# Row maxima of the attention scores taken as minima of negated scores

## The chip, the cores and the metric

The kernel runs on one core of one Trainium2 chip. The metric is the device time of one execution in microseconds (us). Engines: TensorE (PE; its weight loads are PEld), VectorE (DVE), ScalarE (ACT), GpSimd (POOL) and SyncE (SP), which issues nearly all DMAs here.

## The reference, cut to what matters

Local and global attention, then a two-layer MoE block, then a soft MoE. Only the local attention is touched by the change; with B = 4, H = 8, 512 local and 32 global keys, head dimension 64:

```
def sm(s):
    s = s - np.max(s, axis=-1, keepdims=True)
    e = np.exp(s)
    return e / (np.sum(e, axis=-1, keepdims=True) + 1e-09)
s_ll = scale * q_l @ k_l^T            # masked to |i - j| <= 32 with -1e9
s_lg = scale * q_l @ k_g^T
out_l = sm(concat([s_lg, s_ll])) @ concat([v_g, v_l])
out_g = sm(scale * q_g @ [k_g; k_l]^T) @ [v_g; v_l]
x = concat([out_g, out_l])            # 2176 rows of 512
h = x @ w_in;  g = max(0.01 h, h);  x = g @ w_out      # w_in 512 x 2048
# soft MoE over x: logits x @ phi, two softmaxes, 8 experts (w1, w2)
```

## The kernel before, in words

The attention works on 16 pairs of heads (4 batches, 4 pairs each). For a pair, `a_T` transposes queries and keys (kT, qT) and builds overlapping key windows (kw, L405 and L406), `a_S` makes the scores and the exponentials, `a_E` transposes the exponentials (etp, copied to eT at L477), and `a_V` multiplies by the values (po) and scales into xn (L501). A score tile is 128 queries by 128 keys (a window of 96 local keys and the 32 global ones); a pair has 8 of them, 4 for each head of the pair.

In `a_S` a tile goes through three steps: the scores by TensorE (L434, into sc); a fused instruction of VectorE that adds the mask, writes the sum to se and keeps the row maximum in mx (L446); and the exponential by ScalarE (L454), with the negated maximum nmx as its bias and the row sum kept in sm. Between the second and the third, one negation for the four tiles of a head turns mx into nmx (L452).

The MoE block takes token tiles of 128 rows: `b_X` transposes xn and splits it into a high and a low part (xxh, xxl; xqn and xkn for the third tile, L665 and L666), and `b_H` multiplies by w_in (hp, L689), 12 matmuls for each quarter f of 512 columns. The product with w_out is folded into the router: `p_items` transposes 16 pieces of w_out (wotp, L345), copies them (wt, L347) and multiplies them by phi (ptps, L354). `b_L` transposes the activations (gtp, L726), whose copies are gT (L728).

Both weights arrive as 64-bit integers' words. `fetch` loads a piece of 128 x 512 into a ring of four buffers (rraw, L233), and `convert` makes it 32-bit: two steps on ScalarE (L250, L251), two on VectorE (L253, L257) and one on GpSimd (L261), behind which the buffer is free again. A piece of w_in is then split into wi by a cast on ScalarE (L307) and a subtraction on GpSimd or VectorE (L308).

What sets the order: the program is written as lists of items that `merge` interleaves by weights written in the source, and the framework's scheduler then orders the instructions of each engine by a simulated timeline of its own. Each engine runs its own list strictly in order. In the opening (the attention of the first batch, with the pieces of w_in) TensorE also runs matmuls of the identity (`warm`, L85) that compute nothing.

Of the kernel before, what the change touches and what calls it, by code (L numbers as in the profile page):

```python
# [8 lines left out]
F32 = mybir.dt.float32  # L9
# [4 lines left out]
AF = mybir.ActivationFunctionType  # L14
ALU = mybir.AluOpType
# [5 lines left out]
def kernel(  # L21
# [15 lines left out]
    nc = tc.nc  # L37
# [4 lines left out]
    P = 128  # L42
    NT = S // P
# [7 lines left out]
    scale = 1.0 / float(D) ** 0.5  # L51
# [7 lines left out]
    def bank(tag, name, bufs):  # L59
        return ps.tile([P, 512], F32, tag=tag, name=name, bufs=bufs)  # L60
# [9 lines left out]
    with tc.tile_pool(name="id", bufs=1) as idp:  # L70
# [6 lines left out]
        out=s44[:, 0, :], in_=ident.rearrange("p (g s) -> p s g", g=4), axis=AX.X, op=ALU.add  # L77
# [5 lines left out]
    def warm(t):  # L83

        nc.tensor.matmul(  # L85
            t, identr, identr.unsqueeze(1).to_broadcast([P, 4, P]), start=True, stop=True
        )
# [24 lines left out]
    sa = actx.enter_context(tc.tile_pool(name="sa", bufs=2))  # L112
# [23 lines left out]
    for r in range(2):  # L136
        nc.gpsimd.affine_select(
            out=em4[:, r, :], in_=em4[:, r, :], compare_op=ALU.is_ge, fill=0.0,
# [3 lines left out]
            out=em4[:, r, :], in_=em4[:, r, :], compare_op=ALU.is_ge, fill=0.0,  # L142
# [269 lines left out]
    def win(u):  # L412
        return min(max(u - 1, 0), NW - 1)
# [3 lines left out]

    def a_S(b, i):
        qt, kw = qT.pop((b, i)), kwin.pop((b, i))
        mx = sa.tile([P, 2, NT], F32, tag="mx", name="mx", bufs=2)  # L420
        nmx = sa.tile([P, 2, NT], F32, tag="nmx", name="nmx", bufs=2)
        sm = sa.tile([P, NT, 2], F32, tag="sm", name="sm", bufs=2)
        rs = sa.tile([P, NT, 2], F32, tag="rs", name="rs", bufs=2)
        es = []
        bks = [bank("sc", f"sc{e}", 2) for e in range(2)]
        if b == 0:
            for bk in bks:
                warm(bk)
        seq_ = [(T, u, e) for T in range(NT) for u in range(4) for e in range(2)]
        for T, u, e in seq_ if b > 1 else sorted(seq_, key=lambda x: x[2]):  # L430
            U = 4 * T + u
            if True:
                if True:
                    last_a[0] = nc.tensor.matmul(  # L434
                        bks[e][32 * u:32 * u + 32, P * T:P * T + P],
                        qt[64 * e:64 * e + 64, 32 * U:32 * U + 32],
                        kw[win(U) // (NW // 2)][64 * e:64 * e + 64, win(U) % (NW // 2), :],
                        start=True, stop=True,
                    ).ins
        for e in range(2):  # L440
            bk = bks[e]
            s = sa.tile([P, S + SG], F32, tag="se", name="se", bufs=4)[:, 0:S].rearrange(
                "p (t k) -> p t k", t=NT
            )
            for T in range(NT):
                nc.vector.tensor_tensor_reduce(  # L446
                    out=s[:, T, :], in0=bk[:, P * T:P * T + P],
                    in1=mask[:, 0 if T == 0 else 2 if T == NT - 1 else 1, :],
                    scale=1.0, scalar=-3.0e38, op0=ALU.add, op1=ALU.max,
                    accum_out=mx[:, e, T:T + 1],  # L450
                )
            nc.vector.tensor_scalar_mul(nmx[:, e], mx[:, e], -1.0)  # L452
            for T in range(NT):
                exp_last[0] = nc.scalar.activation(  # L454
                    out=s[:, T, :], in_=s[:, T, :], func=AF.Exp,
                    bias=nmx[:, e, T:T + 1], accum_out=sm[:, T, e:e + 1],
                ).ins
            es.append(s)
        nc.vector.tensor_scalar_add(sm, sm, 1e-9)
        nc.vector.reciprocal(rs, sm)  # L460
        sc[b, i] = (es, rs)
# [166 lines left out]
    def step(n):  # L628

        b, i = order[n]  # L630
        last = i == NP - 1
        e = (0.9, lambda: a_E(b, i))
        v = (1.6, lambda: (a_V(b, i), None if n < NP else load_vn(b) if i == NP - 2 else load_v(n + (1 if last else 2))))
        ns = [(2.7, lambda: a_S(*order[n + 1]))] if n + 1 < NN else []
        nt = [(0.9, lambda: T_(n + 2))] if n + 2 < NN else []
        if not last:
            gs = [(2.2, lambda: g_S(b))] if i == NP - 2 else []
            return ns + [e] + gs + nt + [v]
        gv = (2.1, lambda: (g_V(b), load_v(n + 2) if b else None))
        return [e, (0, lambda: None), v, (1.1, lambda: g_E(b))] + ns + nt + [gv]  # L640
# [368 lines left out]
    g_prep(kgn, kgT, 1.0)  # L1009
    T_(0)  # L1010
    a_S(*order[0])
    T_(1)
    st0, st1, st2, st3 = (step(n) for n in range(NP))
# [37 lines left out]
    with tc.issue_after(raw_last[0]):  # L1051
        load_vn(0)
    s4, s5, s6, s7 = (step(n) for n in range(NP, 2 * NP))
    h3 = [(2.6, lambda f=f: b_H(3, f)) for f in range(NQ)]
    merge(pit, hs[3] + [(2.1, lambda: (g_V(0), load_v(NP)))] + [
        (0.9, lambda: T_(NP)), (2.7, lambda: a_S(*order[NP])), (0.9, lambda: T_(NP + 1))
    ] + s4[:2] + [(0.5, lambda: b_X(3))] + h3[:2] + s4[2:-1])
    pctx.close()
# [30 lines left out]
    for n, t in enumerate(wo2):  # L1089
        nc.sync.dma_start(  # L1090
            out=t, in_=wo_f[512 * n:512 * n + 512, :].rearrange("(k p) f -> p k f", p=P)
# [217 lines left out]
    for m, (c0, c1) in enumerate(((0, CL), (CL, 512))):  # L1309
        W = c1 - c0  # L1310
        sop = bank(("po", "sm")[m], "sop", 1)[:, 0:W]
        for k in range(KF):
# [8 lines left out]
            out=so[:, c0:c1], in0=so0[:, c0:c1], in1=sop, op=ALU.add  # L1321
# [3 lines left out]
        if m == 0:  # L1325
# [3 lines left out]
            out=sst[64:128, c0:c1], in0=sp[64:128], in1=sst[64:128, c0:c1], op=ALU.subtract  # L1329
# [4 lines left out]
        for n, ts in enumerate(order2):  # L1334
# [11 lines left out]
            if len(ts) == 1:  # L1346
# [3 lines left out]
                    out=out.rearrange("(b r) c -> b r c", b=B)[:, 0:SG, c0:c1], in_=ob  # L1350
                )
            else:
                ob = obp.pop(0).rearrange("p (t c) -> p t c", c=W)
                copy(ob, opv)
                b, T = seq[ts[0]]
                r0 = ROWS * b + SG + P * T
                (nc.scalar if m and nop % 2 else nc.sync).dma_start(
                    out=out[r0:r0 + G * P, c0:c1].rearrange("(t p) c -> p t c", p=P), in_=ob
# [36 lines left out]
```

## Time and profile before

| what | us |
|---|---|
| median of 3 runs | 491.11 (490.76 to 493.39) |
| the profiled execution | 492.57 |
| its span, first to last instruction | 490.8 |
| TensorE busy | 458.0 (93%) |
| VectorE busy | 274.7 (56%) |
| ScalarE busy | 232.7 (47%) |
| GpSimd busy | 160.1 (33%) |

The granted clock of TensorE is 0.974 of full speed over the span, and 0.66 from 25 to 50 us. A row of the timeline gives the start, the duration of the row, the engine, the line, what is written from what, and in brackets how long the engine was idle before and what ended that. Durations of neighbours overlap, since an instruction starts before the last one's end is through.

### The profile page before, as it was taken

How to read it: one execution, taken by the hardware profiler on the slowest of the kernel's cores; microseconds unless marked ns; L12 is line 12 of the kernel's file. 1: busy time of each engine (PE TensorE's matmuls, PEld its weight loads, DVE VectorE, ACT ScalarE, POOL GpSimd, SP SyncE). 2: the span in 40 equal slices, each digit the busy share in tenths (PEclk: the TensorE clock that was granted, in tenths of full speed). 3: DMA queues.
4: the chain of work that ended last, by engine and by line, in shares of the span. 5: the costliest groups of instructions: out<-in, count | busy, mean ns of one | idle time of the engine just before them, and what ended most of it. 6: DMA issues, size and time to landing. Idle time of an engine off the chain costs nothing.

```text
span 490.8 us, 13457 instructions
## 1 busy us (share of the span) xinstructions
PE 458.0 (93%) x5341; PEld 318.5 (65%) x5341; DVE 274.7 (56%) x880; ACT 232.7 (47%) x678; POOL 160.1 (33%) x281
## 2 busy tenths in 40 slices
PE   7968789998989999999999999999999999999982
PEld 5646568675767666776777776777777777743341
DVE  4676879488557676466554656435755542242223
ACT  4666889477854445444155526123533343321021
POOL 2044887333310202642515251515766630000000
PEclk9985899999999999999999999999999999999998
DMA  9989688499665565443450221229720049999997
GB/s 178 220 201 244 206 271 331 158 294 294 206 164 109 132 130 93 95 104 92 99 107 1 59 46 16 87 99 397 278 86 1 2 164 346 392 348 398 348 308 248
DMA packets 111990, 90.23 MB, mean 184 GB/s; under 512 B 75256, under 2 KB 94392, under 8 KB 111928
## 3 DMA queue, kind: packets, MB, share of 16 engines
q1 hardware_dynamic: 110024, 88.33, 61.8%
q10 hardware_dynamic: 1904, 1.05, 0.8%
q8 instruction: 42, 0.69, 0.6%
q14 instruction: 20, 0.16, 0.1%
HBM read 76.68 MB, written 8.65 MB: 174 GB/s over the span
## 4 chain that ended last, share of the span: by engine, by line
PE 74%; DMA 9%; ACT 6%; SPq 4%; DVE 4%; issue 1%; POOL 1%; DVEq 0%; ACTq 0%; POOLq 0%
PE hp L689 37%; DMA rraw<-in_moe_w_in_dram 5%; PE gtp L726 4%; PE sc L434 3%; PE up L810 3%; PE ehp L1259 3%; PE po L493 3%; PE lg L740 3%; PE etp L473 2%; DMA rraw<-in_moe_w_out_dram 2%; PE sop L1293 1%; SPq L162 1%; ACT se L454 1%; PE gpo L579 1%; PE qTp L390 1%
## 5 line engine op out<-in xcount | busy, mean ns | idle before, releaser
L689 PE MATMUL hp<-wi,xxh 128*128 128x512 f32 x512 | 166.9, 407 | 1.3 <-ACT xxh L665 1.3
L689 PEld LDWEIGHTS hp<-wi,xxh 128*128 128x128 f32 x512 | 91.7, 190 | 28.3 <-issue 8.2
L717 POOL COPY g<-gb 32x256 f32<-32x256 f32 x206 | 82.6, 401 | 81.4 <-DVE gb L708 54.3
L689 PE MATMUL hp<-wi,xxl 128*128 128x512 f32 x256 | 101.4, 397 | 0.2 <-DVE xxl L666 0.2
L696 ACT ACTIVATE g<-hp 128x512 f32<-128x512 f32 x60 | 35.3, 595 | 56.2 <-PE hp L689 54.2
L454 ACT ACTIVATE se<-se,nmx 128x128 f32<-128x128 f32 x128 | 49.6, 390 | 22.5 <-DVE nmx L452 22.5
L689 PEld LDWEIGHTS hp<-wi,xxl 128*128 128x128 f32 x256 | 48.5, 189 | 13.0 <-issue 1.7
L200 POOL COPY vw<-vw 32x1664 f32<-32x1664 f32 x10 | 15.8, 1576 | 79.6 <-DMA vw<-in_v_g_dram 26.7
L446 DVE CUSTOM_DVE_ANT_0 se<-sc,mask 128x128 f32<-128x128 f32 x128 | 28.8, 283 | 12.1 <-PE sc L434 12.0
L261 POOL TENSOR_TENSOR wn<-wn,rraw 128x512 int32<-128x512 int32 x16 | 22.9, 1436 | 36.9 <-DVE wn L257 31.1
L708 DVE STREAM_TRANSPOSE gb<-g 128x512 f32<-128x512 f32 x32 | 22.2, 702 | 18.7 <-ACT g L696 13.4
L434 PE MATMUL sc<-kw,qT 64*32 64x128 f32 x1024 | 29.2, 283 | 1.5 <-ACT rraw L251 0.6
L261 POOL TENSOR_TENSOR wo<-wo,rraw 128x512 int32<-128x512 int32 x12 | 15.7, 1310 | 33.0 <-DVE wo L257 9.6
L434 PEld LDWEIGHTS sc<-kw,qT 64*32 64x32 f32 x1024 | 19.9, 109 | 9.5 <-issue 5.4
L493 PE MATMUL po<-vw,eT 128*32 128x64 f32 x1024 | 23.8, 228 | 1.2 <-issue 1.0
L477 DVE COPY eT<-etp 128x512 f32<-128x512 f32 x28 | 18.6, 684 | 10.0 <-PE etp L473 10.0
L454 ACT ACTIVATION_READ_ACCUMULATOR se<-se,nmx 128x1 f32 x128 | 24.1, 188 | 0.0
L473 PE MATMUL etp<-identr,se 128*128 128x128 f32 x128 | 23.1, 301 | 0.3
L493 PEld LDWEIGHTS po<-vw,eT 128*32 128x32 f32 x1024 | 17.8, 113 | 8.1 <-issue 6.8
L405 DVE COPY kw<-kT 128x672 f32<-128x672 f32 x32 | 19.8, 652 | 2.9 <-ACT kT L394 2.7
L251 ACT ACTIVATE rraw<-rraw 128x512 int32<-128x512 uint32 x28 | 18.7, 677 | 5.0 <-DMA rraw<-in_moe_w_out_dram 3.8
L473 PEld LDWEIGHTS etp<-identr,se 128*128 128x128 f32 x128 | 16.0, 148 | 6.6 <-ACT se L454 2.8
(228 smaller groups left out, 765.3 us busy)
## 6 DMA issues: line engine op xcount, KB each, us to landing
ew<-in_moe_w_dram SPq DMA_DIRECT2D x23, 1024.0 KB, 8.2
rraw<-in_moe_w_in_dram SPq DMA_DIRECT2D x16, 512.0 KB, 6.1
ew<-in_moe_w_dram SPq DMA_DIRECT2D x15, 512.0 KB, 8.8
vw<-in_v_l_dram SPq DMA_DIRECT2D x60, 112.0 KB, 3.3
rraw<-in_moe_w_out_dram SPq DMA_DIRECT2D x12, 512.0 KB, 6.6
wo_f<-wo SPq DMA_DIRECT2D x16, 256.0 KB, 3.8
vn<-in_v_l_dram SPq DMA_DIRECT2D x4, 1024.0 KB, 6.3
wo<-wo_f SPq DMA_DIRECT2D x4, 1024.0 KB, 7.7
```

Of the source, the lines that this page charges most:

```text
L261: nc.gpsimd.tensor_tensor(out=di, in0=di, in1=m, op=ALU.add)
L405: nc.vector.tensor_copy(kw[:, :, 0:96], src)
L434: last_a[0] = nc.tensor.matmul(bks[e][32 * u:32 * u + 32, P * T:P * T + P], qt[64 * e:64 * e + 64, 32 * U:32 * U + 32], kw[win(U) // (NW / ...
L446: nc.vector.tensor_tensor_reduce(out=s[:, T, :], in0=bk[:, P * T:P * T + P], in1=mask[:, 0 if T == 0 else 2 if T == NT - 1 else 1, :], sca ...
L454: exp_last[0] = nc.scalar.activation(out=s[:, T, :], in_=s[:, T, :], func=AF.Exp, bias=nmx[:, e, T:T + 1], accum_out=sm[:, T, e:e + 1],).ins
L473: last_a[0] = nc.tensor.transpose(pt[:, P * T:P * T + P], es[e][:, T, :], ident).ins
L493: last_a[0] = nc.tensor.matmul(pov[32 * u:32 * u + 32, T, e, :], ets[e][:, 32 * U:32 * U + 32], vw[:, win(U), e, :], start=True, stop=True ...
L689: nc.tensor.matmul(hp, a[:, k, :], w[c][:, k, :], start=(k == 0 and n == 0), stop=(k == KD - 1 and n == 2),)
L696: nc.scalar.activation(out=gs, in_=hp, func=AF.Prelu, alpha=0.01)
L708: nc.vector.transpose(out=gb[:, f % 2], in_=gs)
L717: copy(dst[32 * c:32 * c + 32, :, a], src[32 * a:32 * a + 32, :, c])
L726: nc.tensor.transpose(pt[:, P * c:P * c + P], g[:, o:o + P], ident)
```

## The change

The fused instruction gets a scale of -1 and a minimum in place of the maximum: it writes the negated masked scores, and the minimum of these, kept directly in nmx, is the negated maximum. The tile mx and the 32 negations (16 pairs, 2 heads each) go. The exponential multiplies its input by -1.

```
--- before.py
+++ after.py
@@ -417,7 +417,6 @@
 
     def a_S(b, i):
         qt, kw = qT.pop((b, i)), kwin.pop((b, i))
-        mx = sa.tile([P, 2, NT], F32, tag="mx", name="mx", bufs=2)
         nmx = sa.tile([P, 2, NT], F32, tag="nmx", name="nmx", bufs=2)
         sm = sa.tile([P, NT, 2], F32, tag="sm", name="sm", bufs=2)
         rs = sa.tile([P, NT, 2], F32, tag="rs", name="rs", bufs=2)
@@ -446,13 +445,12 @@
                 nc.vector.tensor_tensor_reduce(
                     out=s[:, T, :], in0=bk[:, P * T:P * T + P],
                     in1=mask[:, 0 if T == 0 else 2 if T == NT - 1 else 1, :],
-                    scale=1.0, scalar=-3.0e38, op0=ALU.add, op1=ALU.max,
-                    accum_out=mx[:, e, T:T + 1],
+                    scale=-1.0, scalar=3.0e38, op0=ALU.add, op1=ALU.min,
+                    accum_out=nmx[:, e, T:T + 1],
                 )
-            nc.vector.tensor_scalar_mul(nmx[:, e], mx[:, e], -1.0)
             for T in range(NT):
                 exp_last[0] = nc.scalar.activation(
-                    out=s[:, T, :], in_=s[:, T, :], func=AF.Exp,
+                    out=s[:, T, :], in_=s[:, T, :], func=AF.Exp, scale=-1.0,
                     bias=nmx[:, e, T:T + 1], accum_out=sm[:, T, e:e + 1],
                 ).ins
             es.append(s)
```

The order of the instructions changes as well, since the scheduler orders the program anew. Line numbers behind L420 are lower by one or two in the changed program.

The first place is ScalarE, 60 to 64 us, the arrival of the last pieces of w_in. cv is a piece's high word, g the activation of the first tile, xqn the high part of the third token tile. Before:

```order
L307 CAST wi<-wn 128x512
L251 ACTIVATE rraw<-rraw 128x512
L250 ACTIVATE cv<-rraw 128x512 x2
L251 ACTIVATE rraw<-rraw 128x512
L307 CAST wi<-wn 128x512
L696 ACTIVATE g<-hp 128x512
L665 ACTIVATE xqn<-xtp 128x512
L307 CAST wi<-wn 128x512 x2
```

and of the change:

```order
L307 CAST wi<-wn 128x512
L251 ACTIVATE rraw<-rraw 128x512
L250 ACTIVATE cv<-rraw 128x512
L694 ACTIVATE g<-hp 128x512
L250 ACTIVATE cv<-rraw 128x512
L251 ACTIVATE rraw<-rraw 128x512
L663 ACTIVATE xqn<-xtp 128x512
L307 CAST wi<-wn 128x512 x2
```

The cast L307 that stood ahead of xqn now stands behind it, and the activation is one step nearer.

The second place is VectorE, 42 to 53 us. The rows with cv are pieces 5, 6 and 7 of w_in; xn is the product of the attention of the third and fourth head pair. Before:

```order
L257 SCALAR_TENSOR_TENSOR wn<-rraw,wn 128x512
L501 TENSOR_TENSOR xn<-po,rs 128x4x128
L459 TENSOR_SCALAR sm<-sm 128x8
L477 COPY eT<-etp 128x512
L253 TENSOR_SCALAR cv<-cv 128x512
L460 RECIPROCAL rs<-sm 128x8
L257 SCALAR_TENSOR_TENSOR wn<-rraw,cv 128x512
L253 TENSOR_SCALAR cv<-cv 128x512
L257 SCALAR_TENSOR_TENSOR wn<-rraw,cv 128x512
L253 TENSOR_SCALAR cv<-cv 128x512
L501 TENSOR_TENSOR xn<-po,rs 128x4x128
L257 SCALAR_TENSOR_TENSOR wn<-rraw,cv 128x512
```

and of the change:

```order
L257 SCALAR_TENSOR_TENSOR wn<-rraw,wn 128x512
L475 COPY eT<-etp 128x512
L457 TENSOR_SCALAR sm<-sm 128x8
L458 RECIPROCAL rs<-sm 128x8
L253 TENSOR_SCALAR cv<-cv 128x512
L499 TENSOR_TENSOR xn<-po,rs 128x4x128
L475 COPY eT<-etp 128x512
L257 SCALAR_TENSOR_TENSOR wn<-rraw,cv 128x512
L253 TENSOR_SCALAR cv<-cv 128x512
L257 SCALAR_TENSOR_TENSOR wn<-rraw,cv 128x512
L499 TENSOR_TENSOR xn<-po,rs 128x4x128
L253 TENSOR_SCALAR cv<-cv 128x512
```

The first shift (L253) of cv has moved ahead of the first xn, while its second step (L257) stays behind that and the copy eT.

The third place is ScalarE, 134 to 142 us, the last pieces of w_out; the exponentials are those of the seventh head pair. Before:

```order
L250 ACTIVATE wo<-rraw 128x512
L347 COPY wt<-wotp 128x512 x2
L454 ACTIVATE se,sm<-se,nmx 128x128 x4
L347 COPY wt<-wotp 128x512
L454 ACTIVATE se,sm<-se,nmx 128x128 x4
L728 COPY gT<-gtp 128x512 x2
L361 ACTIVATE pmat<-ptps 128x128
```

and of the change:

```order
L250 ACTIVATE wo<-rraw 128x512
L347 COPY wt<-wotp 128x512
L452 ACTIVATE se,sm<-se,nmx 128x128 x7
L347 COPY wt<-wotp 128x512
L452 ACTIVATE se,sm<-se,nmx 128x128
L726 COPY gT<-gtp 128x512 x2
L361 ACTIVATE pmat<-ptps 128x128
```

Before, four exponentials stood ahead of the last copy wt; now there are seven.

## Rows read from the trace of the kernel before

**Rows 1.** The page's first part: busy us, share of the span, instructions.
```profile
PE 458.0 (93%) x5341; PEld 318.5 (65%) x5341; DVE 274.7 (56%) x880; ACT 232.7 (47%) x678; POOL 160.1 (33%) x281
```

**Rows 2.** Busy time by stretch: length, engines' busy us (instructions), clock, DMA share, GB/s.
```profile
0.00:65.00 65.00, 51.05 (x658) 35.95 (x658) 43.34 (x145) 44.21 (x123) 26.93 (x37) 0.84 0.94 210
65.00:200.00 135.00, 129.72 (x1687) 92.41 (x1687) 94.96 (x295) 84.83 (x244) 44.70 (x42) 1.00 0.71 196
200.00:425.00 225.00, 224.41 (x2415) 164.60 (x2413) 115.42 (x392) 92.12 (x283) 88.48 (x204) 1.00 0.40 125
425.00:491.00 66.00, 52.77 (x584) 25.55 (x584) 20.95 (x51) 11.58 (x29) 0.00 (x0) 0.96 0.96 334
```

**Rows 3.** The timeline from 44 to 56 us, four engines, rows picked.
```profile
44.21 0.61 ACT L250 ACTIVATE cv<-rraw 128x512 f32<-128x512 f32 x1
...
46.59 0.69 DVE L501 TENSOR_TENSOR xn<-po,rs 128x512 f32<-128x512 f32 x1 [2.92 <-PE po L493]
...
48.45 0.69 DVE L253 TENSOR_SCALAR cv<-cv 128x512 uint32<-128x512 uint32 x1
...
49.10 0.65 ACT L250 ACTIVATE cv<-rraw 128x512 f32<-128x512 f32 x1 [1.53 <-DMA rraw<-in_moe_w_in_dram]
...
49.99 2.72 POOL L261 TENSOR_TENSOR wn<-wn,rraw 128x512 int32<-128x512 int32 x2 [2.72 <-DVE wn L257]
...
53.91 3.04 POOL L261 TENSOR_TENSOR wn<-wn,rraw 128x512 int32<-128x512 int32 x2
...
55.71 0.33 SPq L233 DMA_DIRECT2D rraw<-in_moe_w_in_dram  x1
```

**Rows 4.** Groups by line: busy us, mean ns of one; idle before, releaser.
```profile
L446 DVE CUSTOM_DVE_ANT_0 se<-sc,mask 128x128 f32<-128x128 f32 x128 | 28.8, 283 | 12.1 <-PE sc L434 12.0
...
L452 DVE TENSOR_SCALAR nmx<-mx 128x4 f32<-128x4 f32 x32 | 7.8, 258 | 0.2
...
L454 ACT ACTIVATE se<-se,nmx 128x128 f32<-128x128 f32 x128 | 49.6, 390 | 22.5 <-DVE nmx L452 22.5
```

**Rows 5.** The negation's line: durations in ns, least, median, longest.
```profile
L452 DVE TENSOR_SCALAR nmx<-mx x32: 149/164/1250, 14.5 to 295.3; 128x4 f32<-128x4 f32 x32
```

**Rows 6.** The timeline from 62 to 65 us, TensorE and ScalarE.
```profile
62.50 0.60 PE L607 MATMUL gtp<-identr,gn 128*128 128x128 f32 x4
62.77 0.60 ACT L307 CAST wi<-wn 128x512 fp32r<-128x512 f32 x1
63.28 0.59 ACT L696 ACTIVATE g<-hp 128x512 f32<-128x512 f32 x1
63.77 0.59 ACT L665 ACTIVATE xqn<-xtp 128x512 fp32r<-128x512 f32 x1
...
64.41 0.73 PE L689 MATMUL hp<-wi,xqn 128*128 128x512 f32 x2 [1.31 <-ACT xqn L665]
```

**Rows 7.** The timeline from 137 to 143 us, three engines.
```profile
137.82 1.08 PE L434 MATMUL sc<-kw,qT 64*32 64x128 f32 x32
...
139.52 0.59 ACT L347 COPY wt<-wotp 128x512 f32<-128x512 f32 x1
...
140.16 1.06 PE L354 MATMUL ptps<-wt,phis 128*32 128x128 f32 x26 [0.34 <-ACT wt L347]
...
141.17 0.69 DVE L501 TENSOR_TENSOR xn<-po,rs 128x512 f32<-128x512 f32 x1 [1.07 <-PE ptps L354]
...
141.78 0.68 DVE L728 COPY gT<-gtp 128x512 f32<-128x512 f32 x1
...
142.51 0.66 PE L726 MATMUL gtp<-identr,g 128*128 128x128 f32 x4 [1.29 <-DVE gT L728]
```

**Rows 8.** The timeline at 40 us, VectorE and ScalarE: a long negation.
```profile
39.83 1.21 DVE L452 TENSOR_SCALAR nmx<-mx 128x4 f32<-128x4 f32 x1
...
41.07 0.40 ACT L454 ACTIVATE se<-se,nmx 128x128 f32<-128x128 f32 x1 [1.40 <-DVE nmx L452]
```

**Rows 9.** The ring's sends of w_out from 90 to 125 us.
```profile
L233 SPq DMA_DIRECT2D rraw<-in_moe_w_out_dram x8: 328/372/1481, 93.3 to 123.5; - x8
```

More of the change, by code (lines that the diff above doesn't have):

```diff
@@ L419, in a_S @@
         qt, kw = qT.pop((b, i)), kwin.pop((b, i))
-        mx = sa.tile([P, 2, NT], F32, tag="mx", name="mx", bufs=2)
         nmx = sa.tile([P, 2, NT], F32, tag="nmx", name="nmx", bufs=2)
@@ L448, in a_S @@
                     in1=mask[:, 0 if T == 0 else 2 if T == NT - 1 else 1, :],
-                    scale=1.0, scalar=-3.0e38, op0=ALU.add, op1=ALU.max,
-                    accum_out=mx[:, e, T:T + 1],
+                    scale=-1.0, scalar=3.0e38, op0=ALU.add, op1=ALU.min,
+                    accum_out=nmx[:, e, T:T + 1],
                 )
-            nc.vector.tensor_scalar_mul(nmx[:, e], mx[:, e], -1.0)
             for T in range(NT):
                 exp_last[0] = nc.scalar.activation(
-                    out=s[:, T, :], in_=s[:, T, :], func=AF.Exp,
+                    out=s[:, T, :], in_=s[:, T, :], func=AF.Exp, scale=-1.0,
                     bias=nmx[:, e, T:T + 1], accum_out=sm[:, T, e:e + 1],
```

## The prediction

> **What bounds the kernel now.** I read the page's first part, then the busy time by stretch. TensorE is busy for 458.0 of 490.8 us [rows 1]. By stretch [rows 2] it lacks 13.95 us in the first 65, 5.28 from 65 to 200, 0.59 from 200 to 425, and the rest in the tail. Three quarters of the kernel is therefore matmul behind matmul, and what another engine saves beside a busy TensorE is worth nothing. The tail from 425 moves as a whole: DMA is at 0.96 there, but its weight loads go into buffers that TensorE's work frees. What this change can move is two things: when TensorE's steady stream begins, and how many short waits stand in it between 65 and 200. The part before 65 is held by the pieces of the first weight, which come by DMA through a ring of four buffers and are converted by ScalarE, VectorE and GpSimd in turn. I call them pieces 1 to 16; the one that ScalarE takes at 49.10 is piece 6, and the one at 44.21 piece 5 [rows 3].
>
> **What goes, and its price.** There are 32 negations, 7.8 us of VectorE time [rows 4], most of them 0.16 us long and one 1.25 [rows 5]. VectorE is busy for 274.7 us of the span [rows 1], so this is 3% of an engine with 216 us to spare. From 65 us on TensorE's matmuls cover it. With that cover gone the price would be the 7.8 us at most; I take zero.
>
> The trace shows neither of the new forms, the minimum in the reduction and the scale of -1 in the exponential. The nearest rows are the old forms, 128 each, of 0.283 and 0.390 us [rows 4], with the same operands and element counts. If each new form were 0.1 us off, either way, it would be 12.8 us on each of two engines that are half idle, again beside TensorE. I take no difference, and price even that at under 1 us either way, since only the opening would show it.
>
> A second effect: a tile's exponential now needs its own reduction alone, not the fourth of its group and a negation: one 0.16 and up to three reductions of 0.283 less, some 0.8 to 1.0 us earlier for a group's first exponential, where ScalarE is free. ScalarE waits 22.5 us for the negations in all [rows 4]; all but the opening's share of it lies beside a busy TensorE.
>
> **What moves.** The scheduler orders the program anew around these savings. I follow the two places where the waits of TensorE are longest.
>
> *The start of the stream.* TensorE ends a group of transposes at 63.10 (62.50 + 0.60) and waits 1.31 us for the copy xqn, the third token tile's high part, which ScalarE starts at 63.77 [rows 6]. Ahead of xqn on ScalarE, behind the arrival of piece 11, stand conversions, a cast (L307) and an activation. In the changed order that cast stands behind xqn. From its start at 62.77 to the next at 63.28 it is 0.51 us [rows 6]. Piece 11 itself was sent at 55.71, when GpSimd had freed piece 7's buffer, the first of the two in the row at 53.91; before that it did pieces 5 and 6 in 2.72 us from 49.99 on [rows 3]. Piece 5 came that late because its VectorE shift, at 48.45, stood behind the product xn, which had waited 2.92 us for TensorE; ScalarE had delivered the piece at 44.82 (44.21 + 0.61) [rows 3]. Now the shift stands ahead of xn, and the attention work before it has lost its negations, so piece 5 leaves GpSimd before piece 6, which lands at 49.10, needs it. Half of the 2.72, or 1.36 us, goes from GpSimd's list ahead of piece 7, but piece 6 passes VectorE no more than a few tenths sooner. So piece 11 is sent between 0 and 1.36 us earlier; I take 0.5, nearer the low end, because piece 6's landing is the nearest row. Together xqn is 1.0 us earlier. Bounds: at best the whole wait of 1.31 goes; at worst the four exponentials that now stand ahead of a conversion of piece 3 (4 x 0.390) push a later piece by 1.6. I take -1.0.
>
> *The end of the second weight's pieces, at 139 us.* TensorE waits 0.34 us for a copy wt and then 1.29 for a copy gT [rows 7]. Let E be 138.90, the end of the last score matmuls (137.82 + 1.08). Before, wt started after four exponentials, at E + 0.62, and the products that need it ran from E + 1.26. Now seven exponentials stand ahead of wt, and the seventh needs the third reduction of the last group: 3 x 0.283 after E, then 0.390 of its own and 0.59 of wt, so the products start at about E + 1.8, half a microsecond later. They take 1.06. Behind them on VectorE stand xn (0.69), two small steps (some 0.3, a sum and a reciprocal like those beside them) and gT (0.68) [rows 7], so gT is done at about E + 4.5. The transposes behind that wait ran from 142.51, with the next group able to follow at 143.17, or E + 4.3, and it is that next group which needs gT now. This place loses 0.2 us. Bounds: it gains the 1.63 of both waits if all is ready, and loses 1.0 if the two delays add. I take +0.2.
>
> *The other waits between 65 and 200.* 5.28 in all, less the 1.63 of that place, leaves 3.65 us. Their places keep their kind, but each hangs on an order that has changed. I see no sign: zero, with -3.65 and +3.65 as the ends.
>
> **The sum.** -1.0 + 0.2 = -0.8 us. The profiled execution took 492.57 us, its span of 490.8 and 1.8 around it, so 491.8 on its own terms. It lay 1.46 above the median of the runs, 491.11; for the median the forecast is 490.3.
>
> **A rule weighed.** One negation took 1.21 us where 0.16 is usual, and the exponential behind it waited 1.40 [rows 8]; the longest took 1.25 [rows 5]. The Trainium skill, page "SBUF — State Buffer", section "Who interferes with whom", says that a VectorE instruction in a two-port mode and a GpSimd instruction take an exclusive lock on a shared pair of ports, and the other blocks for the whole instruction. By that rule such a wait leaves with its instruction, and what stands next, if it is not of that kind, starts at once. By the rows alone the two cost 2.1 us (1.05 and 1.09) more than the others would.
>
> **Rivals.**
> *Faster: the two held negations were on the path.* If what delayed pieces 3 to 5 was those two, the start gains 2.1 us more: 488.2 us. For it: both lie before 41.1, in the stretch that ends TensorE's slow opening, and ScalarE's next work waited for one of them. Against it: ScalarE still waits 1.53 us at 49.10 for piece 6's DMA [rows 3], so a lead won before that is lost there, and the next copies on VectorE can be held in the same way. The same time comes out if over half of the 3.65 us of other waits goes.
> *Slower: exponentials hold back the second weight's pieces.* The place is 93 to 143 us, where 8 pieces of the second weight are sent between 93.3 and 123.5 [rows 9]. Exponentials that become ready one by one are now put ahead of conversions and of wt on ScalarE. If one piece misses its turn in the ring, TensorE waits for one spacing: 30.2 / 7 = 4.3 us, and with the terms above the time is 494.6. It decides from the point where a piece is later than the work that is queued ahead of its transposes. For it: TensorE waits for wt already at 140.16, so the reserve there is gone. Against it: the loads and conversions of this stretch keep their order but for a few places.
> *It does nothing:* negations off the path and an order of equal worth give 491.1, inside the forecast's own case.
>
> **Chances.** The forecast's case, 488.7 to 493.5, has 0.60; faster 0.22; slower 0.18. A measurement of this kernel tells about 0.5% (2.5 us) from no change, so these cases are also the three chances. The range, 487.5 to 494.6, takes in the points of both rivals; the terms' own ends (-1.31 - 1.63 - 3.65 and +1.6 + 1.0 + 3.65) reach a little further, and all of them at once I leave out.
>
> **What would show it.** Right: the third tile's first matmuls start near 63.4 in place of 64.41; TensorE's lack from 65 to 200 is again 4 to 7 us; 200 to 425 is as full as before; the two groups of reductions and exponentials last 0.28 and 0.39. Wrong: a start of that tile before 62 or after 65, a new wait of over 2 us between 93 and 143, or a minimum form that lasts longer than the maximum form.

## The result, and the profile after

The change makes the kernel slower. In the first comparison its median is 497.48 us (496.3 to 498.32, 4 runs) against 492.25 of before (490.76 to 493.39, 4 runs), a ratio of 1.0106 [1.0063, 1.0149]. Run again beside other kernels it is 497.01 against 492.21, 1.0082 [1.0054, 1.0110]. The forecast was 490.3, with 494.6 as the upper end of its range. The profiled execution took 496.3 us, its span 494.6; that is 3.7 us over before's profiled one, where the medians differ by 4.8 to 5.2, so the two profiles show a little less than the whole loss.

The page of the changed kernel, first part and the two groups that answer to [rows 1, 4]:

```profile
PE 458.9 (93%) x5341; PEld 319.8 (65%) x5341; DVE 268.5 (54%) x848; ACT 234.2 (47%) x678; POOL 158.6 (32%) x281
...
L452 ACT ACTIVATE se<-se,nmx 128x128 f32<-128x128 f32 x128 | 49.8, 392 | 19.8 <-DVE nmx L445 19.5
L445 DVE CUSTOM_DVE_ANT_0 se<-sc,mask 128x128 f32<-128x128 f32 x128 | 28.8, 284 | 13.1 <-PE sc L433 13.0
```

The negations are gone: VectorE has 848 instructions for 880 and 6.2 us less to do. The new forms last 0.284 and 0.392 us, the old ones 0.283 and 0.390. ScalarE even waits 2.7 us less for the row maxima. None of this is where the time went.

Busy time by stretch, columns as in [rows 2]:

```profile
0.00:65.00 65.00, 49.71 (x661) 35.68 (x662) 42.69 (x137) 45.01 (x125) 26.00 (x37) 0.87 0.97 215
65.00:200.00 135.00, 128.24 (x1620) 91.27 (x1619) 89.84 (x279) 84.33 (x241) 41.78 (x35) 0.97 0.71 191
200.00:425.00 225.00, 224.61 (x2441) 164.86 (x2441) 114.61 (x382) 91.62 (x281) 90.81 (x211) 1.00 0.39 121
425.00:495.00 70.00, 56.33 (x622) 28.01 (x620) 21.38 (x52) 13.24 (x32) 0.00 (x0) 0.96 0.96 333
```

From 65 to 200 TensorE has done 1620 matmuls where it had done 1687, and its clock is 0.97, not 1.00. The 225 us behind are as full as before. So the loss is made before 200 us. The places where the prediction looked, TensorE and its releasers; this answers to [rows 6, 7]:

```profile
62.25 0.61 ACT L663 ACTIVATE xqn<-xtp 128x512 fp32r<-128x512 f32 x1
62.91 1.22 PE L687 MATMUL hp<-wi,xqn 128*128 128x512 f32 x2 [2.69 <-ACT xqn L663]
...
104.08 0.66 PE L345 MATMUL wotp<-identr,wo 128*128 128x128 f32 x4
...
138.79 1.08 PE L433 MATMUL sc<-kw,qT 64*32 64x128 f32 x32 [0.35 <-DVE nmx L445]
...
139.80 0.66 PE L345 MATMUL wotp<-identr,wo 128*128 128x128 f32 x4
...
141.43 0.56 ACT L347 COPY wt<-wotp 128x512 f32<-128x512 f32 x1
...
142.05 1.91 PE L354 MATMUL ptps<-wt,phis 128*32 128x128 f32 x26 [1.59 <-ACT wt L347]
143.40 0.69 DVE L499 TENSOR_TENSOR xn<-po,rs 128x512 f32<-128x512 f32 x1 [2.54 <-DMA wo_f<-wo]
143.94 0.59 ACT L726 COPY gT<-gtp 128x512 f32<-128x512 f32 x1 [1.54 <-PE ptps L354]
...
144.58 1.12 PE L724 MATMUL gtp<-identr,g 128*128 128x128 f32 x4 [0.62 <-ACT gT L726]
...
170.79 0.66 PE L724 MATMUL gtp<-identr,gx 128*128 128x128 f32 x4 [0.28 <-ACT gs L540]
```

The third tile's matmuls start at 62.91, 1.5 us earlier than the 64.41 of [rows 6]. The transposes at 104.08, though, were at 104.02 before: by then the lead is gone. The last products are at 142.05 (before 140.16, [rows 7]): 1.9 late. The transposes of gx at 170.79 were at 167.52: 3.3 late. The span ends 3.8 later. TensorE's clock in windows of 2 us, the seventh number behind the length:

```profile
62.00:64.00 2.00, 1.09 (x3) 0.72 (x4) 1.81 (x4) 2.00 (x5) 0.74 (x1) 0.60 0.74 213
64.00:66.00 2.00, 2.00 (x7) 1.57 (x7) 1.82 (x3) 2.00 (x5) 2.00 (x2) 0.55 0.80 253
66.00:68.00 2.00, 2.00 (x10) 1.64 (x9) 1.36 (x2) 1.22 (x3) 2.00 (x3) 1.00 0.93 304
...
142.00:144.00 2.00, 1.91 (x26) 1.34 (x26) 0.60 (x1) 0.46 (x3) 0.00 (x0) 0.50 1.00 277
144.00:146.00 2.00, 1.42 (x10) 0.91 (x10) 1.13 (x5) 0.74 (x2) 0.00 (x0) 0.50 1.03 273
```

Behind both waits, of 2.69 and 1.59 us, TensorE runs at the lower of its two levels, 1.2 in place of 2.4 GHz. The 26 products last 1.91 for 1.06. In the trace of before all these windows stand at 1.00.

### The profile page after: what moved, and what is told of

Read it like the earlier page. It is cut to its first block, busy times and chain, and to the rows that moved or that the text cites. A ratio compares the mean times of both kernels' runs of the same rounds, so it can differ in the third digit from the quotient of the medians.

```text
span 494.6 us, 13428 instructions
## 1 busy us (share of the span) xinstructions
PE 458.9 (93%) x5341; PEld 319.8 (65%) x5341; DVE 268.5 (54%) x848; ACT 234.2 (47%) x678; POOL 158.6 (32%) x281
## 4 chain that ended last, share of the span: by engine, by line
PE 75%; DVE 4%; DMA 4%; ACT 3%; issue 1%; SPq 1%; POOL 0%; DVEq 0%; ACTq 0%; POOLq 0%
PE hp L687 38%; PE gtp L724 4%; PE sc L433 3%; PE up L808 3%; PE ehp L1257 3%; PE po L491 3%; PE lg L738 2%; PE etp L471 2%; PE sop L1291 1%; PE gpo L577 1%; PE qTp L390 1%; PE sop L1313 1%; PE lg L912 1%; DMA wo_f<-wo 1%; PE xtp L657 1%; PE gl L517 1%
## 5 line engine op out<-in xcount | busy, mean ns | idle before, releaser
L261 POOL TENSOR_TENSOR wn<-wn,rraw 128x512 int32<-128x512 int32 x16 | 21.9, 1376 | 36.2 <-DVE wn L257 30.4
L491 PE MATMUL po<-vw,eT 128*32 128x64 f32 x1024 | 25.1, 234 | 5.8 <-DMA vw<-vw 4.2
L471 PE MATMUL etp<-identr,se 128*128 128x128 f32 x128 | 21.9, 291 | 0.2
L726 ACT COPY gT<-gtp 128x512 f32<-128x512 f32 x26 | 14.8, 588 | 11.1 <-PE gtp L724 8.6
```

The costliest lines, as they stand in the source:

```text
L261: nc.gpsimd.tensor_tensor(out=di, in0=di, in1=m, op=ALU.add)
L471: last_a[0] = nc.tensor.transpose(pt[:, P * T:P * T + P], es[e][:, T, :], ident).ins
L491: last_a[0] = nc.tensor.matmul(pov[32 * u:32 * u + 32, T, e, :], ets[e][:, 32 * U:32 * U + 32], vw[:, win(U), e, :], start=True, stop=True ...
```

## The experiments

All were timed in five rounds beside the kernel before, whose median lay between 492.2 and 493.0. In the diffs, `tc.issue_after(x)` puts the instructions of its block behind x on x's engine. "Early" means that a head's exponentials come free one by one, "held" that they come free together.

**The forms, VectorE's work, or the order.** First the changed kernel again, and the new forms with a product by 1 where the negation was. The latter gives every engine the order of before.

```
+            nc.vector.tensor_scalar_mul(nmx[:, e], mx[:, e], 1.0)      # e1; minima go to mx
```

> The changed kernel, run again beside the experiments. Both theories: 1.0 to 1.5% over the kernel before, with TensorE's wait for xqn of 2 to 3 us near 62 and a wait for wt of 1.4 us or more near 141, and the granted clock at 0.5 behind each of the two.

> New forms (minimum, scale -1) with a product by 1 where the negation stood, so that every engine's list of instructions is in the order of the kernel before. Theory O (the new order costs the time, the forms cost nothing): 0.998 to 1.002 of the kernel before, groups of 0.283 and 0.390 us as there. Theory F (the forms cost: a slower minimum, or a slower exponential): 1.005 or more, with longer means in one of the two groups.

e0 took 497.01 us, a little less of a loss than expected (0.8%), and its wait for xqn was 1.64 us, not 2 to 3. e1 took 492.84, a ratio of 0.9996 [0.9974, 1.0019]: minimum, scale of -1 and all cost nothing. The mirror image has the old forms and no negation, in the order of the changed kernel; the bias then has the wrong sign, so the exponentials' values differ.

```
+                    scale=1.0, scalar=-3.0e38, op0=ALU.add, op1=ALU.max,
+                    out=s[:, T, :], in_=s[:, T, :], func=AF.Exp,
```

> Old forms (maximum, scale 1) without the negation, in exactly the order of the changed kernel; the exponential takes the maximum with the wrong sign as its bias, which is the part that is left out. Theory O: the changed kernel's time within 0.3%, 1.010 or more of the kernel before, with the two waits and the two stretches at clock 0.5. Theory F: the time of the kernel before, within 0.3%.

496.88 us, 1.0086 [1.0058, 1.0115]: the order alone costs what the change costs. (In its profile the clock stayed at 1.00 behind the wait for wt, which I had not expected.) A third run puts the 32 products back on VectorE, but into a tile that nothing reads.

```
+            nc.vector.tensor_scalar_mul(dd[:, e], nmx[:, e], 1.0)
```

> Changed kernel with the 32 products by 1 put back on VectorE into a tile that nothing reads: VectorE has the work of before, no exponential waits for it. ScalarE's order is the changed kernel's but for five copies, VectorE's and TensorE's local places differ. Theory O (order by early release): as the changed kernel, 496 to 497.8. Rival (VectorE's relief itself moved the order or the time): under 495.

496.87 us, 1.0071 [1.0045, 1.0098]. VectorE's relief is worth nothing that can be measured. What is left is that exponentials come free early and the scheduler deals with them in another way.

**Early against held.** Each head's exponentials start with the fourth tile's, and the other three stand behind it; there is no negation.

```
+            for T in (3, 0, 1, 2):
+                with tc.issue_after(lead) if lead else ExitStack():   # lead: the first exponential
```

> Changed kernel in which a head's four exponentials start with the fourth tile's and the other three stand behind it, so that they come free together, as they did behind the negation; there is no negation. The order of the instructions is a third one, neither before's nor the changed kernel's. Theory E (it is the early release of single exponentials that spoils the order): the time is before's, 491 to 493.5. Rival (any order that is not the one for which the weights of the lists were chosen loses at some wait of its own): 494.5 to 498, with new waits at other places than 63 and 142 us.

493.23 us, 1.001 [0.9987, 1.0034]: the loss is gone, in an order that is not that of before. The counterpart leaves three of four exponentials early, in a fourth order.

```
+                    accum_out=(mx if T in (3,) else nmx)[:, e, T:T + 1],
+            nc.vector.tensor_scalar_mul(nmx[:, e, 3:4], mx[:, e, 3:4], 1.0)
```

> Changed kernel with a product by 1 on VectorE (one column, 32 instructions, as many as the negations) between the fourth tile's minimum and its exponential, so that only the first three exponentials of a head come free early; the order is a fourth one. If early release of exponentials is what the scheduler makes bad orders of: 495.5 to 498, with a wait for wt over 1 us near 142. If the order of before and of e7 were only two good draws and orders scatter, the time is anywhere, 490 to 498, and its waits are elsewhere.

496.97 us, 1.0077 [1.0049, 1.0104], with a wait of 1.59 us for wt at 142.57. The two held orders (that of before, and e7) are level, the early ones (the changed kernel's, e10, e11) slow. That speaks against a mere draw of orders, though five are few.

**Where: parts held.** The condition of e7 for some pairs only (b counts batches, i pairs in a batch).

```
+            held = b == 0              # e8;  e9: b > 0;  e12: (b, i) == (1, 1);  e15: b == 0 and i < 2
```

> The edit of e7_held_exps for the first batch alone (the pairs worked on before about 65 us); behind them single exponentials come free early, as in the changed kernel. The two parts of that edit move instructions at disjoint places, so this run and e9_held_late together are e7. Theory P (the loss is made from 104 us on, by what stands ahead of the last pieces of w_out): the way from the transposes wotp at 104.08 to gtp at 170.79 stays at 66 to 67.8 us, with a wait for wt near 1.6, and the median at 496 to 497. Theory S (the loss is made in the opening): 492.5 to 493.5.

> The same edit for all batches but the first: the opening is the changed kernel's, single exponentials and the order around xqn included; from the second batch on a head's four exponentials come free together. Theory P: the way from 104 to gtp is 62.9 to 63.7 us as in e7 and before, no wait for wt over 0.4, and the median is at 492 to 493.5. Theory S: 496 to 497.

> Changed kernel with the exponentials of the sixth head pair alone held together (8 of 128); the opening is the changed kernel's, and the lists differ from it only between about 113 and 150 us and in some transfers. In the new lists the last copy wt stands behind five exponentials, not seven, and the conversion of the last piece of w_out one copy earlier. Theory P (late half: the loss stands around the last pieces of w_out): the way from the transposes wotp at 104 to gtp at 170.79 falls from 66.3 (mean of seven profiles) to under 64.8, and the median to 494.5 to 495.3. Rival (the late loss is spread over many pairs): above 496.

> Changed kernel with the exponentials of the first two head pairs held together (16 of 128); from 65 us on it is the changed kernel's order. ScalarE's order of conversions and casts in the opening becomes that of before. If the opening's half of the loss is made by these 16 exponentials pushing conversions of the pieces 2 to 5: as e8_held_open, 494.6 to 495.4. If it takes all four pairs of the batch: 496 to 497.

e8 took 495.01 us, 1.0044 [1.002, 1.0067], and e9 494.75, 1.0029 [1.0005, 1.0054]: each half gives back about 2 us, so neither theory alone was right. The size is loose, since the intervals of e0 and e8 overlap. e12 took 493.69, 1.0012 [0.9985, 1.0039], more than I had given it: holding eight exponentials of 128, those of the sixth pair, with what the scheduler moves around them, takes back over 3 of the some 4 us. e15 took 497.2, 1.0077 [1.0046, 1.0108]: the first two pairs give nothing back. The gains do not add up (2 us for the opening, over 3 for the sixth pair, about 4 for all); e9 holds the sixth pair too, but in its order gT waits 2.36 us at 144 and TensorE is at half clock behind it. e12's trace at the late place:

```profile
134.13 1.30 POOL L261 TENSOR_TENSOR wo<-wo,rraw 128x512 int32<-128x512 int32 x1 [2.18 <-PE po L495]
...
136.76 1.29 POOL L261 TENSOR_TENSOR wo<-wo,rraw 128x512 int32<-128x512 int32 x1 [1.33 <-PE sc L433]
...
138.72 0.66 PE L345 MATMUL wotp<-identr,wo 128*128 128x128 f32 x4
...
139.59 0.56 ACT L347 COPY wt<-wotp 128x512 f32<-128x512 f32 x1
...
140.20 1.06 PE L354 MATMUL ptps<-wt,phis 128*32 128x128 f32 x26 [0.49 <-ACT wt L347]
```

and the last two pieces of w_out in the changed kernel, on GpSimd:

```profile
132.48 1.29 POOL L261 TENSOR_TENSOR wo<-wo,rraw 128x512 int32<-128x512 int32 x1 [3.16 <-DVE wo L257]
137.18 1.29 POOL L261 TENSOR_TENSOR wo<-wo,rraw 128x512 int32<-128x512 int32 x1 [3.41 <-DVE wo L257]
```

What matters is the gap between the last two pieces: 4.70 us in the changed kernel, 2.63 with the sixth pair held. In before it is 3.54 (132.72 and 136.26). It is the gap between the first steps of their conversions on ScalarE (L250): 130.30 and 134.99 in the changed kernel, 131.74 and 134.39 in e12, 130.54 and 134.09 in before. In the changed kernel the last of these stands behind a copy wt that waits for its transposes:

```profile
134.50 0.59 ACT L347 COPY wt<-wotp 128x512 f32<-128x512 f32 x1 [0.22 <-PE wotp L345]
134.99 0.69 ACT L250 ACTIVATE wo<-rraw 128x512 f32<-128x512 f32 x1
```

In e12, as in before, it stands ahead of that copy:

```profile
134.39 0.67 ACT L250 ACTIVATE wo<-rraw 128x512 f32<-128x512 f32 x1
135.26 0.59 ACT L347 COPY wt<-wotp 128x512 f32<-128x512 f32 x1 [0.20 <-PE wotp L345]
```

In e12 the last copy wt, too, comes 0.9 us behind the start of its transposes (138.72 to 139.59), not 1.6 (139.80 to 141.43). The wait for wt is 0.49 for 1.59, and the clock stays at 1.00.

**What of the late place.** Only the copy wt is moved, ahead of the seventh pair's last four exponentials; all other lists are the changed kernel's.

```
+            late = (b, i, e) == (1, 2, 1)
             for T in range(NT):
+                with tc.issue_after(wt_last[0]) if late else ExitStack():
...
```

> The changed kernel with one step moved: on ScalarE the last copy wt stands ahead of the last group's exponentials (four ahead of it, not seven); all other lists are the same. Theory O, by its second place: the wait for wt of 1.6 us falls to about 0.5, the clock stays at 1.0 there, and 1.5 to 2.5 us come back, 0.3 to 0.5% less than the changed kernel. Rival (the 139 us place is a symptom of pieces of w_out that come late, 116 to 138): another wait takes its place, and under 0.7 us come back.

```profile
142.91 1.91 PE L354 MATMUL ptps<-wt,phis 128*32 128x128 f32 x26 [0.68 <-ACT wt L347]
145.44 1.12 PE L727 MATMUL gtp<-identr,g 128*128 128x128 f32 x4 [0.62 <-ACT gT L729]
```

496.86 us, 1.0087 [1.0059, 1.0116]. The wait fell as expected, from 1.59 to 0.68, and nothing came back that can be measured: in this profile the products still run at half clock, behind a wait of only 0.68. Neither expectation fits, since no other long wait took the place of the first. Next, matmuls that keep TensorE busy behind the last transposes. The scheduler then puts these transposes ahead of the last scores.

```
+            if c == 3:
+                for _ in range(6):
+                    with tc.issue_after(wk_last[0]):
+                        wk_last[0] = nc.tensor.matmul(
+                            pt[:, P:4 * P], identr, identr.unsqueeze(1).to_broadcast([P, 3, P]),
...
```

> Changed kernel with six idle matmuls of the identity (384 columns each, into the unused part of the products' bank) behind the last transposes wotp; the scheduler then puts these transposes ahead of the seventh pair's last scores and the last copy wt ahead of its exponentials. Theory C: no wait for wt above 0.4 and the clock at 1.0 from 140 to 148 (the changed kernel: 1.59 us and 0.50 to 0.72); the way from wotp at 104.08 to the transposes gtp at 170.79 falls from 66.7 toward before's 63.5, by 2 to 3 us, and the median to 494.4. Rival L: the scores only move behind and their own chain of reduction, exponential and transposes becomes the wait; under 0.8 us comes back.

```profile
140.51 1.12 PE L346 MATMUL wotp<-identr,wo 128*128 128x128 f32 x4 [2.63 <-POOL wo L261]
```

497.71 us, 1.0123 [1.0089, 1.0158]: theory C fell, and rival L names another chain than the one that came. The transposes now wait 2.63 us for GpSimd's last piece (139.18), and the clock falls behind that wait. In the changed kernel they stand behind the scores and wait for nothing. So the piece leaves no room to run the transposes earlier; that it delays the changed kernel itself, e5 does not show.

**What of the opening.** Six idle matmuls ahead of the third tile's, and then both edits.

```
+                for _ in range(6):
+                    wk_last = nc.tensor.matmul(
+                        wk, identr, identr.unsqueeze(1).to_broadcast([P, 4, P]), start=True, stop=True
...
+            with tc.issue_after(wk_last):
+                b_H(t, 0)
```

> Changed kernel with six idle matmuls of the identity (512 columns each, into a free bank) put ahead of the third token tile's first matmuls, where TensorE waits for xqn (2.69 us in the changed kernel's trace, granted clock 0.50 to 0.60 behind it). Theory C (the clock): the lead of 1.5 us at xqn is eaten because TensorE runs at half clock behind that wait; with the wait filled the clock stays at 1.0 from 62 to 70, and the way from the start of the xqn matmuls to the transposes wotp that stood at 104.08 falls from 41.2 to 39.6, before's; the median falls from 496.9 by 1.2 to 2.0, to about 495.3. Rival L (the list): the lead is lost anyway, to waits for the second product's pieces or the activation g a few us later; the clock rises but the way to 104 stays near 41 and the median within 0.6 of 496.9.

> Both edits together. Theory C: the two gains add, 3.2 to 5 us, and the median is at 492 to 493.5, as before's 492.2. Rival L: 495.5 or more.

```profile
63.77 0.73 PE L688 MATMUL hp<-wi,xqn 128*128 128x512 f32 x2 [0.42 <-ACT xqn L663]
...
81.30 0.44 PE L345 MATMUL wotp<-identr,wo 128*128 128x128 f32 x2 [1.88 <-POOL wo L261]
```

The rows are e4's. It took 499.62 us, 1.0152 [1.0121, 1.0182], e6 499.54, 1.0152 [1.0111, 1.0193]. The clock did stay at 1.00 from 62 to 70, yet e4 is some 2 to 3 us slower than the changed kernel, which neither theory forecast. The edit itself is in the way: the idle matmuls last 1.54 us (61.37 to 62.91), and the scheduler put two transposes of w_out's first piece 12 matmuls ahead, where TensorE waits 1.88 us for that piece on GpSimd. In the changed kernel these transposes wait for nothing (81.50). So e4 and e6 do not show what the lead is lost to.

The other profiles say more on the clock. In e3, e9, e11, e12 and e13 it stayed at 1.00 from 60 to 76, and the way from xqn's matmuls to the transposes that stood at 104.08 takes 41.3 to 42.7 us. In the changed kernel, e0, e2 and e10 it fell near xqn's wait, and the way takes 41.2 to 42.5. In before and e1, where it stayed up, it takes 39.6 and 39.4. So in these profiles the half clock is not what the opening loses.

Next, the wait itself: xqn in e9's order is moved ahead of a conversion whose piece had not landed.

```
+            with tc.issue_after(xq_ins[0]) if (f, k) == (2, 3) else ExitStack():
+                win_s.next(w, cv)
```

> e9_held_late with the copy xqn ahead of the conversion of the 12th piece of w_in on ScalarE (and that conversion's followers moved with it); TensorE's and GpSimd's lists are those of e9. In e9 this conversion waited 1.74 us for its DMA, and xqn and two casts behind it. Theory X (the opening's loss is xqn and the casts behind an unarrived piece): TensorE's wait for xqn falls under 0.5 us and the median from 494.75 to 492.8 to 493.8. Rival W (the opening's loss is that of the stream of pieces through GpSimd, which comes to the first piece of w_out 2.1 us later in the seven orders with early exponentials): the wait goes, the time stays above 494.2.

494.69 us, 1.0024 [0.9993, 1.0055]: the wait for xqn is gone from TensorE's list (xqn's matmuls start at 62.31), the time is e9's 494.75. That speaks for rival W, but the interval does not shut out the 1 to 2 us of theory X; and TensorE's next long wait, 1.48 us at 76.24, is for an activation g. In the profiles GpSimd starts its first piece of w_out at 77.62 to 81.01, 79.0 on average, in the seven orders whose opening is that of before or held (before, e1, e7, e8, e14, e16, e17). In the ten early openings (the changed kernel, e0, e2, e3, e5, e9 to e13) it starts at 79.56 to 82.06, 80.8 on average (e4, e6 and e15 are left out). So the stream of pieces comes later in the early openings, though one order alone spreads over 3.4 us (before, e1 and e16). Between the two kernels' own orders the difference is smaller: 79.5 for before, e1 and e16, 80.4 for the changed kernel, e0, e2 and e3. Which step of the stream falls back is not settled.

**A version that beats both.** In e7 TensorE's longest wait behind 65 us is for gT:

```profile
140.30 0.69 DVE L502 TENSOR_TENSOR xn<-po,rs 128x512 f32<-128x512 f32 x1 [1.81 <-DMA wo_f<-wo]
...
140.91 0.68 DVE L729 COPY gT<-gtp 128x512 f32<-128x512 f32 x1
...
141.64 0.66 PE L727 MATMUL gtp<-identr,g 128*128 128x128 f32 x4 [1.82 <-DVE gT L729]
```

gT stands behind the product xn, and xn waits for the last store of w_out. e14 exchanges the two rows; e17 is the same kernel again, e16 the same exchange in the kernel before.

```
+        with tc.issue_after(g_ins[2, 1]) if (b, i) == (1, 0) else ExitStack():
+            nc.vector.tensor_tensor(
...
```

> e7_held_exps with two rows of VectorE exchanged: the copy gT ahead of the product xn at 140 us. In e7 xn waits there 1.81 us for the last store of w_out (DMA wo_f), gT stands behind it, and TensorE waits 1.82 for gT. If that is so: the wait for gT falls under 0.5 and the median from 493.2 to 491.4 to 492.2, below both kernels. If another wait takes its place (the copy pmat, the products lg): 493.

> The kernel before, negations and all, with the same two rows of VectorE exchanged as in e14 (gT ahead of xn); all other lists are before's. If e14's gain over before is this exchange alone: 489.5 to 491, level with e14 on the same chip, and the wait of 1.29 us for gT at 141 falls under 0.7. If the freed negations and the third order carry part of it: 491.2 to 492.5, at least 1 us above e14.

> e14_gT_ahead once more, beside e16 on the same chip: 489.5 to 490.8.

e14's rows at the same place:

```profile
137.20 1.06 PE L354 MATMUL ptps<-wt,phis 128*32 128x128 f32 x26 [0.34 <-ACT wt L347]
138.18 0.69 DVE L731 COPY gT<-gtp 128x512 f32<-128x512 f32 x1 [1.25 <-PE ptps L354]
...
138.93 0.66 PE L729 MATMUL gtp<-identr,g 128*128 128x128 f32 x4 [0.67 <-DVE gT L731]
...
139.65 0.69 DVE L504 TENSOR_TENSOR xn<-po,rs 128x512 f32<-128x512 f32 x1 [0.58 <-DMA wo_f<-wo]
```

e14 took 489.98 us, 0.9934 [0.9907, 0.9961], and again, as e17, 490.45, 0.9955 [0.9939, 0.9971]: faster than both kernels, and e14 by more than expected. TensorE's wait is 0.67, not under 0.5: gT itself must wait for the products. e16 took 492.98, 0.9995 [0.9977, 1.0012]: its wait fell from 1.29 to 0.67 and gave nothing that can be measured, where both expectations had a gain. So the exchange pays in the held order without negations, where xn stood in front with a wait of 1.81 for the store; that it should give 3 us for 1.15 of wait is not explained by the profiles. The way from 104 to the transposes of gx is 1.1 to 1.2 us shorter in e14 and e17 than in e7, and the clock stayed at 1.00 there in all three.

The legs of TensorE's list, from the single profile of each kernel (A: the transposes wotp at 104.02 in before; G: those of gx at 167.52; gap: between the starts of the last two pieces on GpSimd; clock: granted clock, lowest 2-us window from 140 to 148):

| kernel | A | gap | G - A | clock | median |
|---|---|---|---|---|---|
| before | 104.02 | 3.54 | 63.50 | 1.00 | 492.25 |
| e1, order of before | 101.97 | 3.54 | 63.65 | 1.00 | 492.84 |
| changed | 104.08 | 4.70 | 66.71 | 0.50 | 497.48 |
| e2, old forms | 105.22 | 4.70 | 64.51 | 1.00 | 496.88 |
| e3, wt first | 105.90 | 4.70 | 66.03 | 0.50 | 496.86 |
| e7, all held | 103.52 | 2.63 | 62.93 | 1.00 | 493.23 |
| e15, first two held | 106.35 | 4.70 | 65.02 | 1.00 | 497.2 |
| e8, opening held | 102.40 | 4.70 | 67.04 | 0.50 | 495.01 |
| e9, rest held | 105.62 | 2.63 | 64.78 | 0.50 | 494.75 |
| e12, sixth held | 104.96 | 2.63 | 62.22 | 1.00 | 493.69 |
| e14, held, gT ahead | 102.02 | 2.63 | 61.70 | 1.00 | 489.98 |

Of the runs not in the table, e0, e4 and e10 (gap 4.70, clock fallen) have legs of 67.19, 65.80 and 66.61, and e13 (gap 2.63, clock fallen) one of 66.28. With a gap of 4.70 the leg is 64.5 to 65.0 where the clock stayed up and 65.8 to 67.2 where it fell; with the shorter gap and the clock up it is 61.7 to 63.7. So, by single profiles, the order costs some 1 to 2 us there by itself, and the clock 1 to 2.5 more in the executions in which it falls. A short gap alone does not suffice: e9 and e13 have it, but wait 2.36 and 2.30 us for gT and fall to half clock there.

## Why the prediction was wrong

Two terms of the sum failed: the start of the stream, priced as a gain of 1.0 us, and the place at 139 us, priced at a loss of 0.2. Together they were a loss of some 3 to 4 us; with 1.0 more of other waits that is about the 4.8 to 5.2 measured.

*The new forms and the negations*, at nothing: right. e1, e2 and e11 show it. The gain of 2.1 us that the faster rival saw in the two held negations did not come: in e1 and e11 products of the negation's kind are held as well, for up to 1.26 and 1.37 us, and each kernel takes the time of its order.

*The start of the stream, -1.0*: the start was right and its sign in the sum wrong. Piece 5 began on GpSimd at 48.22, not at 49.99 as in [rows 3], and xqn's matmuls came 1.5 us earlier; over the profiles of the two orders they came 1.0 earlier, at 63.2 (62.70 to 64.42) for 64.2 (62.59 to 65.64). The lead is no larger than this spread: e1, in the order of before, started at 62.59. The step that failed is the equation of that start with a gain of the whole stream. At 104 TensorE was where it had been. The wait of 2.69 us for xqn and the half clock behind it are not the reason, since openings without the fall take as long from there to 104, and e13, without the wait, takes e9's time within its interval. What comes later is the stream of weight pieces, by 0.9 us over the profiles of the two orders and by 1.8 between all early openings and the others, and holding the first batch gives about 2 us back (e8). So the term was about +1 to +2, around its upper bound of +1.6. Why the stream comes later stays open.

*The place at 139 us, +0.2*: mis-sized. Let E again be the end of the last scores, here 139.87 (138.79 + 1.08). I had the products at E + 1.8; they came at E + 2.18, for E + 1.26 before: 0.9 lost, not 0.5. I then let the transposes behind gT lose almost nothing, since gT would be ready by E + 4.5. They ran at E + 4.71 for E + 3.61: 1.1 lost. What I left out is that TensorE might do all this at half clock: 0.85 more for the products, 0.46 for a group of transposes. I left out as well that the last piece's conversion moves behind a copy wt; with it the gap between the last two pieces grew from 3.54 to 4.70 us. The transposes that stood at 148.43 in before ran at 151.70: 3.3 late, of which 0.97 was there at E. So this place cost 2.3 us in this profile, beyond its bound of +1.0; in e2, where the clock stayed up, the whole leg from 104 is 2.2 us shorter than the changed kernel's.

*The other waits, 0*: the end E itself came 0.97 later (139.87 for 138.90), though TensorE was level at 104. That is inside the bounds of 3.65 but not zero. From 104 to E TensorE has six waits of over 0.3 us, 2.83 in all, where before had two of 1.25 in all; two of the six are for GpSimd's pieces, two for wt.

*The rival that forecast a slower kernel* named the right place and the right mechanism, exponentials that come free one by one and stand ahead of conversions and of wt, and I gave it 0.18. It was priced as one missed turn of the ring, 4.3 us. No turn was missed, and the last piece was sent 1.65 us later (125.16 for 123.51); small delays and the clock made the 3.3 there. The time lies beyond its 494.6 because the -1.0 of the opening, which I kept in that sum, was a loss too, and because the median of before that I started from, 491.11, was itself 1.1 us low (492.25 with one run more). The argument against it, that the loads and conversions keep their order but for a few places, was true and worthless: holding one pair's eight exponentials takes most of the loss back (e12).

Of the signs named in advance two came true on the right side (200 to 425 as full as before, old durations for the new forms). The start of the tile at 62.91, near the 63.4 that I had named as a good sign, was none. None of the signs of being wrong came either: TensorE's longest wait between 93 and 143 was 1.59 us, under the 2 that I had named. The lack of 6.8 us between 65 and 200 lay inside my 4 to 7, since idle time does not show a busy TensorE at half clock.

## What to carry to other kernels

Where a scheduler orders the program, a removed instruction is also a new release time for its readers, and the order that follows can cost more than the instruction did. Time the removal with the old release kept (a held group, a product by 1) before judging it, then mend the one or two waits left. And a wait of TensorE has to be priced with the clock behind it, which fell in some executions of one order and stayed up in others; the length of the wait did not tell which.

## What the runs showed of the hardware

The length of the single wait does not tell whether TensorE's clock falls. The granted clock fell to 0.50 at waits from 0.68 us (e3, 142.91) over 1.59 and 2.36 to 3.51 (e2, 62.70), and stayed at 1.00 behind waits of 2.32 (e3, 64.42), 2.31 (e11, 65.23), 1.88 (e4) and 1.82 (e7). At the same wait of 1.59 for wt it fell in the changed kernel, e0, e4, e8, e10 and e11, and stayed up in e2 and e15. The lower level lasted from some 3 us (at 62.9 in the changed kernel) to some 7 (62 to 69 in e2). The 26 products last 1.91 us at it, for 1.06. The time that one order takes to reach 80 us differs by over 3 us from profile to profile (first piece of w_out at 77.62, 79.81 and 81.01 in the order of before), while from 200 to 425 us TensorE is busy for 224.1 to 224.6 us in every profile read: a difference of 1 us in the opening can't be read from one trace of each kernel.
